# A state-space layer and a feed-forward layer on one core: the weight splits of all eight W_out blocks by ScalarE copies and adding transfers, and a new order from entry 201 on

## The chip, the core and the metric

The kernel runs on one core of one Trainium2 chip. A core has a matrix engine (TensorE; the profile shows its matmuls as PE and its weight loads as PEld), three engines for elementwise work (VectorE or DVE, ScalarE or ACT, GpSimd or POOL) and a synchronising engine (SyncE or SP) that issues most of the transfers. All of them work side by side, each through its own queue in order, and wait for one another by semaphores. The metric is the device time of one execution in microseconds. The kernel before took 329.49 us (median of 3 runs, 328.6 to 329.88).

## What is computed

The reference chains two layers. The first is a state-space scan over 4 batches, 8 heads and 768 positions in float32 (head width 32, state width 16). It works in chunks; within a chunk

```python
M = CB * L                       # L = exp(cum[i] - cum[j]), causal
y_intra = np.einsum('bhij,bhjd->bhid', M, xc)
y_inter = np.einsum('bhin,bhnd->bhid', Cc, state) * decay_to_i[:, :, :, None]
y[:, :, sl] = y_intra + y_inter
state = decay_full[:, :, None, None] * state + np.sum(Bx, axis=2)
```

The result, 3072 tokens of 256 numbers, goes through the second layer, with W_in of 256 x 2048 and W_out of 2048 x 256:

```python
h = x @ w_in
g = h * (1.0 / (1.0 + np.exp(-h)))
return (g @ w_out).astype(np.float32)
```

## The kernel before

**Units and groups.** The scan is cut into twelve units of 256 tokens (u = 0 to 11, three in each batch), and the feed-forward layer into six groups of two units (G or P = 0 to 5). Each weight matrix is cut into eight blocks of 128 x 2 x 256 numbers: blocks 0 to 7 are W_in, blocks 8 to 15 are W_out.

**Split weights.** From group 1 on the feed-forward matmuls run on numbers of a narrower float type, fp32r, and to keep float32 accuracy each weight block and each activation is split into three parts: a high part (`h`), a low part (`l`) and a third part (`d`). For a block n, `lw` loads it, `u` and `v` (ScalarE) and `w` (VectorE, three steps, `w,n,0` to `w,n,2`) and `W` (GpSimd adds, line 318) make the rounded word, `H` (ScalarE, line 322) the high part. The low and third parts can be made in two ways. Either VectorE does both: `lD` (line 326) adds high part and word, `dD` (line 330) makes the third part of high and low part. Or ScalarE and the transfers do: `Wl` and `Wd` (line 335) are ScalarE copies of the high part, plain and scaled, into the places of the low and the third part; `Wm` (line 339) is a transfer, issued from GpSimd's queue, that adds the word onto the low part, and `We` one that adds the low part onto the third. `We` of a block therefore waits until the `Wm` of that block has landed, and GpSimd stands still meanwhile. Before the change blocks 12 to 15 have both parts made by copies and transfers, blocks 10 and 11 the low part only, and blocks 8 and 9 neither: ten transfers.

**The order.** Nothing is scheduled when the kernel is built: a string, `SCHEDULE` (lines 18 to 100), lists 1309 entries such as `q,1,0,1,0`, and a loop at the end of the kernel calls the function of each entry with its numbers. An engine's queue is the entries of that engine in the order of the string. A second table, `SLOTS` (lines 102 to 116), says which place in a pool of equal buffers the next tile of that pool takes (49 places `s2k` of 2 KB a partition, 12 `r4k` of 4 KB, 7 `raw`, 3 PSUM banks `hp`). A tile that takes a place waits until the last user of that place has finished.

**Entries that the text speaks of.** Of the scan: `La`, `Lp`, `Ln`, `Lt`, `Lx` load a unit's inputs (SP); `E` (VectorE scan, line 512), `T` (VectorE transposition of loaded B or C, line 525), `B` and `C` (GpSimd, lines 520 and 551), `ce` (ScalarE, line 546) prepare the operands of `g0` (PE, line 585) and `gd` (PE, line 571); `M` (VectorE, line 600) uses what `g0` made; `b` (ScalarE, line 594) copies what `gd` made, and the four `S` (VectorE, line 615) carry the state over it, `SM` (ScalarE, line 623, twice a unit) masks the states, and `Y` (PE, lines 635 and 644) needs `SM`, `M` and `C`. `y`, `xh` (ScalarE, lines 672 and 679) and `x` (VectorE) then split the result for the feed-forward layer. `AA`, `AP`, `AD` make the decay tables that `La` and `Lp` read; they are on GpSimd except `AP` (VectorE, line 486).

Of the feed-forward layer: group 0 uses plain float32 matmuls for part of its work, `s` (line 697) with `si` (ScalarE, line 703) for W_in and `n1` (line 761) for W_out; an `n1` needs the finished word of its W_out block, an `s` that of its W_in block. With split weights, `a,G,i` (PE, line 800) multiplies by high and low part of block i, `ax` (ScalarE, line 811) rescales the sum in PSUM, `d` (PE, line 800) adds the third part, `dg` (ScalarE, line 821) applies the activation; `h` (ScalarE, line 827), `l` and `e` (VectorE, lines 651 and 837) split the activation, and `q,P,i,k,m` (PE, line 782) is three matmuls by the high, low and third part of W_out block 8 + i, in this order. Scan and feed-forward share two PSUM tiles, `ga` and `gb`. Results are turned by `o` (VectorE, line 715) and stored by `O` (SP).

Of the kernel before, what the change touches and what calls it, by code (L numbers as in the profile page):

```python
# [888 lines left out]
```

## Time and profile before

| what | time |
|---|---|
| median of the three runs | 329.49 us |
| the runs | 328.6, 329.49, 329.88 us |
| the profiled execution | 329.1 us |
| its span, first to last instruction | 327.4 us |
| time around the span (difference) | 1.7 us |
| granted TensorE clock over the span | 0.999 |

The span is the time in which the profile shows instructions. A busy share is the time in which an engine has at least one instruction in work; a PE that is busy all the time has another matmul started before the last has left it. Rows of grouped instructions give the source line, the engine, the operation, what it writes and reads, how often it occurs, its busy time in us and the mean of one in ns. Rows of the stretches give, for a stretch of time, the us in which PE, PEld, DVE, ACT and POOL were busy, with the count of instructions, the granted clock, the share of the 16 DMA engines and GB/s. Rows of the chain of waits and of the timeline begin with the start in us and the duration in us, and end with a count.

### The profile page before, as it was taken

To read this page: it belongs to the slowest core of one execution; us is meant where nothing else is said; L and a number is where in the kernel's file an instruction comes from. 1 tells how busy PE (TensorE), PEld (TensorE's weight loads), DVE (VectorE), ACT (ScalarE), POOL (GpSimd) and SP (SyncE) were. 2 spreads that over 40 slices of the span, in tenths; PEclk is the share of its full clock that TensorE was granted. 3 is DMA by queue.
4 is the path that set the end of the run, shared out by engine and by line. 5 is a ranking of instruction groups with operands and counts; after the bars stand their busy time and mean duration, and the time that the engine had idled before them with its cause. 6 is when DMAs were issued, how large, how long until landed. Compare 5 with 4: busy or idle time off the path is not lost.

```text
span 327.4 us, 7519 instructions
## 1 busy us (share of the span) xinstructions
PE 320.3 (98%) x3064; PEld 243.4 (74%) x3067; DVE 240.4 (73%) x331; ACT 209.5 (64%) x319; POOL 56.0 (17%) x74
## 2 busy tenths in 40 slices
...
GB/s 162 206 200 272 296 175 192 51 148 135 148 127 46 105 115 53 86 36 64 147 74 70 44 1 117 104 26 96 3 74 37 7 2 2 0 88 0 2 1 64
DMA packets 94962, 29.27 MB, mean 89 GB/s; under 512 B 80000, under 2 KB 86912, under 8 KB 94928
## 3 DMA queue, kind: packets, MB, share of 16 engines
...
## 4 chain that ended last, share of the span: by engine, by line
PE 94%; SPq 2%; DMA 1%; DVE 1%; issue 1%; DVEq 0%
PE hp L782 29%; PE ga L800 18%; PE gb L800 18%; PE hp L761 9%; PE hp L697 6%; PE o_ps L782 6%; PE ga L635 2%; PE ga L585 2%; PE ga L644 2%; DMA s2k<-in_C_dram 1%; PE gb L644 1%; PE ga L571 1%; SPq L262 0%; SPq L375 0%; PE o_ps L531 0%
## 5 line engine op out<-in xcount | busy, mean ns | idle before, releaser
L782 PE MATMUL hp<-r4k,s2k 128*128 128x512 f32 x400 | 110.0, 394 | 0.0
L651 DVE SCALAR_TENSOR_TENSOR r4k<-r4k,r4k 128x1024 fp32r<-128x1024 f32 (+1 forms) x42 | 50.5, 1202 | 51.3 <-ACT r4k L827 48.2
L782 PEld LDWEIGHTS hp<-r4k,s2k 128*128 128x128 f32 x400 | 74.0, 188 | 16.4 <-issue 0.3
L800 PE MATMUL ga<-raw,s2k 128*128 128x512 f32 x240 | 62.3, 395 | 0.0
L800 PE MATMUL gb<-raw,s2k 128*128 128x512 f32 x240 | 61.1, 390 | 0.0
L800 PEld LDWEIGHTS ga<-raw,s2k 128*128 128x128 f32 x240 | 44.7, 188 | 11.4 <-ACT ga L811 0.9
L800 PEld LDWEIGHTS gb<-raw,s2k 128*128 128x128 f32 x240 | 44.8, 188 | 9.9 <-ACT gb L811 0.5
L837 DVE SCALAR_TENSOR_TENSOR r4k<-r4k,r4k 128x1024 fp32r<-128x1024 f32 x40 | 49.2, 1231 | 3.4 <-DVE r4k L651 0.9
L827 ACT ACTIVATE r4k<-r4k 128x1024 fp32r<-128x1024 f32 x40 | 42.2, 1058 | 3.2 <-issue 1.3
L811 ACT ACTIVATE ga<-ga 128x1024 f32<-128x1024 f32 x21 | 21.1, 1007 | 24.6 <-PE ga L800 23.8
L811 ACT ACTIVATE gb<-gb 128x1024 f32<-128x1024 f32 x21 | 21.2, 1009 | 17.6 <-PE gb L800 13.3
L782 PE MATMUL o_ps<-r4k,s2k 128*128 128x512 f32 x80 | 30.7, 390 | 0.0
L761 PE MATMUL hp<-r4k,s2k 128*128 128x512 f32 x64 | 30.0, 602 | 0.0
L821 ACT ACTIVATE r4k<-gb 128x1024 f32<-128x1024 f32 x21 | 21.4, 1021 | 12.4 <-PE gb L800 9.9
L520 POOL TENSOR_TENSOR BT<-bn,ab 128x256 f32<-128x256 f32 x10 | 6.7, 672 | 129.5 <-DVE ab L512 123.3
L318 POOL TENSOR_TENSOR s2k<-s2k,s2k 128x512 uint32<-128x512 uint32 (+1 forms) x19 | 23.6, 1250 | 26.4 <-DVE s2k L307 13.7
L821 ACT ACTIVATE r4k<-ga 128x1024 f32<-128x1024 f32 x21 | 21.5, 1023 | 8.4 <-PE ga L800 8.2
L512 DVE TENSOR_TENSOR_SCAN ab<-ab,diag 128x512 f32<-128x512 f32 x20 | 24.8, 1265 | 0.0
L697 PE MATMUL hp<-r4k,s2k 128*128 128x256 f32 x96 | 22.3, 382 | 0.2 <-issue 0.2
L697 PEld LDWEIGHTS hp<-r4k,s2k 128*128 128x128 f32 x96 | 18.0, 190 | 4.0 <-issue 1.4
L761 PEld LDWEIGHTS hp<-r4k,s2k 128*128 128x128 f32 x64 | 11.6, 189 | 10.5 <-issue 9.6
L782 PEld LDWEIGHTS o_ps<-r4k,s2k 128*128 128x128 f32 x80 | 15.0, 188 | 3.2
...
## 6 DMA issues: line engine op xcount, KB each, us to landing
ab<-az SPq DMA_DIRECT2D x20, 256.0 KB, 4.2
...
s2k<-s2k POOLq DMA_DIRECT2D x10, 256.0 KB, 3.8
...
```

The source lines that it names most:

```text
L318: nc.gpsimd.tensor_tensor(out=u[:, :, fs], in0=u[:, :, fs], in1=v[:, :, fs], op=ALU.add)
L512: nc.vector.tensor_tensor_scan(out=o, data0=src, data1=diag.rearrange("p h t -> p (h t)"), initial=0.0, op0=ALU.mult, op1=ALU.add)
L644: nc.tensor.matmul(out=y[w][32 * q:32 * q + 32, c, 64 * k:64 * k + 64], lhsT=xc[64 * c:64 * c + 64, k, h], rhs=m[64 * c:64 * c + 64, k, h] ...
L651: nc.vector.scalar_tensor_tensor(out=l, in0=f32(h), scalar=BACK, in1=y, op0=ALU.mult, op1=ALU.add)
L697: nc.tensor.matmul(out=hp[:, i], lhsT=WT[j][:, kc, 128 * i:128 * i + 128], rhs=XM()[:, 2 * kc:2 * kc + 2, u], start=(kc == 0), stop=(kc == ...
L761: nc.tensor.matmul(out=NP[m], lhsT=WT[8 + f // 2][:, f % 2, 128 * m:128 * m + 128], rhs=GT[0, f // 2][:, f % 2], start=(n == 1), stop=(n = ...
L782: nc.tensor.matmul(out=ACC[P, c], lhsT=WK[8 + i, p][:, k, 128 * m:128 * m + 128], rhs={"h": HT, "l": LT, "d": DT}[p][P, i][:, k], start=(n ...
L800: nc.tensor.matmul(out=o, lhsT=WK[j, q][:, kc, 128 * i:128 * i + 128], rhs=xs[:, 2 * kc:2 * kc + 2], start=(start and q == "h" and kc == 0 ...
L811: nc.scalar.activation(t, t, AF.Copy, scale=1.0 + Z)
L821: nc.scalar.activation(g, t, AF.Silu, scale=BACK)
L827: nc.scalar.activation(t, GT[G, i], AF.Copy, scale=-LESS * Z)
L837: nc.vector.scalar_tensor_tensor(out=DT[G, i], in0=f32(HT[G, i]), scalar=-1.0, in1=f32(LT[G, i]), op0=ALU.mult, op1=ALU.subtract)
```

## The change

Entries 1 to 200 of the order stay. From there on the order is a new one until some 180 us into the execution; the last 323 entries are again those of before. What is done differently in it: the VectorE steps `lD,8`, `lD,9`, `dD,8`, `dD,9`, `dD,10` and `dD,11` are gone, and `Wl,8`, `Wd,8`, `Wl,9`, `Wd,9`, `Wd,10` and `Wd,11` (ScalarE copies) and `Wm,8`, `We,8`, `Wm,9`, `We,9`, `We,10` and `We,11` (adding transfers) take their place. All eight W_out blocks now get low and third part by copies and transfers: sixteen transfers instead of ten. No other work is added or removed; loads, matmuls and stores are the same ones, in another order on every queue. `SLOTS` is changed from the 80th place of `s2k`, the 15th of `r4k`, the 17th of `raw` and the 16th of `hp` on, so that the new order finds free places. No function is changed.

The diff of the order up to the last adding transfer, and of one table of places:

```diff
--- before.py
+++ after.py
@@ -25,94 +25,94 @@
 ce,1,0 g0,1 Lx,1,1,0 Lx,1,0,0 W,4 xh,0 w,5,1 si,0,0 B,1,0 P01,1,1 D,1 s,0,4 M,1,1 lw,1 u,1 lw,12 S,1,0 W,5 v,1 ca S,1,1
 S,1,2 SM,1,0 SM,1,1 lw,13 s,0,5 si,0,5 v,12 C,1 M,1,0 Y,1 w,1,0 w,1,1 W,7 si,0,4 lw,8 w,1,2 W,1,0 z,1 w,12,2 X0,1,0 H,7
 S,1,3 X0,1,1 x,0,0 lD,7 u,12 w,12,0 w,12,1 u,13 w,13,0 w,13,1 W,1,1 s,0,1 u,8 v,8 s,1,5 ir,3 w,8,0 si,0,1 s,1,0 co
-Ln,2,0,1,0 xh,1 W,12 x,1,0 w,8,1 v,13 w,13,2 W,13 lw,15 u,15 w,8,2 Ln,2,1,1,0 si,1,5 s,1,4 a,0,7 si,1,4 n1,9,0 H,12
-Wd,12 x,0,1 lw,14 u,14 n1,11,0 n1,9,1 x,1,1 W,8 Ln,2,1,0,0 v,14 w,14,2 ir,0 si,1,0 n1,1,0 n1,1,1 H,0 n1,0,1 H,1 lw,6 v,6
-w,6,2 n1,11,1 n1,10,1 ir,2 ir,1 u,6 lw,10 Wl,12 AA,0 AA,1 AD,4 w,6,0 AP w,6,1 AD,0 lw,2 Ln,2,0,0,0 ax,0,7 w,15,0 u,10
-u,2 W,6 n1,8,0 AD,1 v,2 H,6 v,10 w,2,0 s,1,1 si,1,1 lw,3 tp,2 dD,7 v,3 v,15 u,3 w,2,1 w,2,2 W,2,0 Lt,3,1,3,0 lD,6 dD,6
-w,14,0 n1,8,1 w,3,2 a,0,6 ax,0,6 w,15,2 W,2,1 s,1,2 si,1,2 H,2 d,0,7 w,14,1 dg,0,7 AD,2 w,3,0 w,15,1 d,0,6 dg,0,6 W,14
-Lt,3,1,0,0 w,10,2 s,0,2 lw,9 u,9 v,9 Lt,3,1,2,0 Lt,3,1,1,0 T,3,1 H,4 si,0,2 n1,10,0 Lx,2,0,0 n1,12,1 La,2,0,0 w,3,1 tq,2
-La,2,1,0 E,2,1 E,2,0 lD,4 w,9,0 W,15 n1,15,1 Lt,3,0,0,0 n1,12,0 B,2 ce,2,0 ce,2,1 Lt,3,0,3,0 g0,2 lw,11 u,11 Lp,2,0 C,2
-M,2,1 Lx,2,1,0 gd,2 b,2,0 b,2,1 S,2,0 S,2,1 H,15 S,2,2 W,3 Lp,3,0 Lt,4,1,1,0 H,13 La,3,1,0 w,10,0 v,11 Lt,4,1,0,0
-n1,15,0 SM,2,0 Wl,15 SM,2,1 w,10,1 W,10 ce,3,1 Lt,4,1,3,0 M,2,0 La,3,0,0 E,3,1 E,3,0 s,0,3 si,0,3 Lt,3,0,2,0 ce,3,0
-n1,13,0 Lt,3,0,1,0 T,3,0 Y,2 Lx,3,1,0 Ln,3,0,0,0 y,2,0 y,2,1 xh,2 x,2,0 n1,5,0 x,2,1 Ln,3,0,1,0 s,1,3 w,9,1 g0,3 C,3 B,3
-M,3,1 Lx,3,0,0 gd,3 b,3,0 b,3,1 S,3,0 S,3,1 Lt,4,0,1,0 w,9,2 n1,0,0 n1,14,1 Lx,4,0,0 Lt,4,0,0,0 La,4,0,0 S,3,2 W,9
-n1,13,1 SM,3,0 M,3,0 SM,3,1 lD,0 Y,3 n1,2,1 n1,3,0 Lt,4,0,3,0 dD,0 La,4,1,0 w,11,0 w,11,1 y,3,0 y,3,1 xh,3 x,3,0 w,11,2
-n1,2,0 W,11 H,10 a,1,0 Wl,10 Wm,10 n1,3,1 n1,4,0 Lt,4,1,2,0 T,4,1 x,3,1 si,1,3 S,3,3 Lp,4,0 C,4 ce,4,1 E,4,0 H,11 ax,1,0
-d,1,0 E,4,1 ce,4,0 Lt,4,0,2,0 n1,5,1 Wl,11 Lx,5,1,0 Wl,13 dg,1,0 n1,4,1 T,4,0 H,8 lD,1 Ln,4,0,0,0 g0,4 lD,2 Ln,4,0,1,0
-B,4 H,9 M,4,1 La,5,1,0 Wm,11 Lx,4,1,0 Wm,12 gd,4 b,4,0 lD,8 b,4,1 dD,1 n1,6,1 h,1,0 S,4,0 S,4,1 Lx,5,0,0 H,3 S,4,2
-SM,4,1 n1,14,0 n1,6,0 SM,4,0 Lt,5,1,3,0 M,4,0 n1,7,0 Vn,0 Y,4 y,4,1 y,4,0 xh,4 l,1,0 n1,7,1 S,4,3 a,1,2 Vn,1 lD,9 dD,8
-dD,2 H,5 a,1,1 ax,1,2 e,1,0 q,1,0,1,0 d,1,2 dD,9 q,1,0,0,1 Ln,5,0,0,0 ax,1,1 d,1,1 Wd,13 Lt,5,1,1,0 q,1,0,0,0 q,1,0,1,1
-AD,3 Lt,5,1,0,0 dD,4 dg,1,2 Lt,5,0,3,0 h,1,2 a,1,4 dg,1,1 h,1,1 Lt,5,1,2,0 T,5,1 ce,5,0 Lt,5,0,2,0 ce,5,1 Lt,5,0,0,0
-lD,3 a,1,3 Lp,6,0 dD,10 o,0,1,2 We,12 dD,3 x,4,1 x,4,0 l,1,2 e,1,2 ax,1,4 d,1,4 H,14 q,1,2,0,1 Ln,5,0,1,0 ax,1,3 d,1,3
-l,1,1 La,5,0,0 E,5,0 dg,1,4 e,1,1 q,1,1,1,1 dg,1,3 Lt,5,0,1,0 h,1,3 q,1,1,0,1 E,5,1 T,5,0 g0,5 B,5 M,5,1 Lp,5,0 C,5 gd,5
-b,5,1 lD,5 Lt,6,1,0,0 b,5,0 S,5,0 Lt,6,1,3,0 S,5,1 Wm,13 We,13 dD,5 q,1,2,1,1 La,6,0,0 q,1,2,0,0 a,1,5 Lx,6,1,0 Wl,14
-ax,1,5 M,5,0 q,1,1,1,0 l,1,3 S,5,2 q,1,1,0,0 SM,5,1 dD,11 La,6,1,0 e,1,3 SM,5,0 d,1,5 h,1,4 dg,1,5 h,1,5 o,0,0,2
-Lt,6,1,2,0 Lt,6,1,1,0 T,6,1 q,1,2,1,0 l,1,4 e,1,4 q,1,3,0,0 l,1,5 e,1,5 q,1,3,1,0 Wd,15 Y,5 E,6,1 Lt,6,0,1,0 y,5,0 y,5,1
-xh,5 q,1,3,1,1 q,1,3,0,1 ce,6,0 Lt,6,0,0,0 a,1,7 ce,6,1 q,1,4,0,0 q,1,5,1,0 Lt,6,0,3,0 ax,1,7 q,1,4,1,0 Lt,7,1,1,0 Wm,15
-We,15 d,1,7 q,1,4,1,1 dg,1,7 Lt,6,0,2,0 Wd,14 q,1,5,1,1 E,6,0 q,1,5,0,1 T,6,0 h,1,7 g0,6 Ln,6,0,1,0 x,5,0 Lx,6,0,0
-Ln,6,0,0,0 B,6 La,7,1,0 M,6,1 gd,6 b,6,1 Lt,7,1,0,0 x,5,1 Wm,14 M,6,0 q,1,4,0,1 a,2,1 b,6,0 ax,2,1 a,1,6 ax,1,6 S,6,0
-S,6,1 Lt,7,0,0,0 C,6 S,6,2 l,1,7 e,1,7 SM,6,1 S,6,3 d,2,1 dg,2,1 SM,6,0 q,1,7,1,0 We,14 d,1,6 dg,1,6 h,1,6 q,1,5,0,0
...
+Ln,2,0,1,0 xh,1 W,12 x,1,0 w,8,1 v,13 w,13,2 W,13 lw,15 u,15 H,0 s,1,4 si,1,4 si,1,5 w,8,2 Ln,2,0,0,0 W,8 lw,2 a,0,7
+n1,9,1 ax,0,7 v,2 si,1,0 u,2 n1,9,0 dD,7 ir,0 x,1,1 H,1 n1,10,0 ir,2 ir,1 AA,0 H,12 Wl,12 n1,1,1 n1,0,1 lw,6 v,6 u,6
+n1,1,0 w,2,0 n1,10,1 w,15,0 w,15,1 w,2,2 AD,4 Lt,3,1,2,0 x,0,1 w,6,0 w,6,1 v,15 n1,8,0 w,15,2 AA,1 AP AD,0 H,5 w,6,2
+n1,8,1 W,6 d,0,7 w,2,1 W,2,1 lw,3 u,3 v,3 w,3,2 w,3,0 s,1,1 Ln,2,1,1,0 Wd,12 lD,0 lw,14 u,14 si,1,1 H,6 H,13 lD,6 v,14
+dg,0,7 n1,11,0 Ln,2,1,0,0 W,2,0 Lt,3,1,1,0 w,14,0 lw,10 tp,2 n1,11,1 Lx,2,0,0 u,10 s,1,2 v,10 si,1,2 w,3,1 W,15 ce,2,1
+H,15 n1,15,0 dD,6 tq,2 La,2,0,0 a,0,6 AD,1 n1,0,0 ce,2,0 ax,0,6 n1,14,0 Wl,13 w,10,0 d,0,6 dg,0,6 H,8 W,3 w,14,1 s,0,2
+w,10,1 si,0,2 La,2,1,0 E,2,1 E,2,0 w,14,2 B,2 Lx,2,1,0 lw,9 u,9 g0,2 Lt,3,1,3,0 v,9 Lt,3,1,0,0 T,3,1 gd,2 b,2,0 b,2,1
+Lp,2,0 C,2 s,0,3 w,10,2 W,14 M,2,1 M,2,0 S,2,0 S,2,1 W,10 w,9,0 La,3,0,0 La,3,1,0 n1,15,1 n1,12,1 ce,3,0 Wd,8 H,10 S,2,2
+SM,2,0 SM,2,1 ce,3,1 n1,5,0 w,9,2 si,0,3 H,4 Ln,3,0,0,0 Wl,8 E,3,0 lw,11 Lt,3,0,1,0 u,11 n1,4,0 w,9,1 W,9 H,3 Y,2 y,2,0
+E,3,1 Lt,4,1,0,0 Lt,3,0,3,0 Lt,3,0,2,0 y,2,1 Ln,3,0,1,0 xh,2 Lt,3,0,0,0 T,3,0 B,3 Lx,3,0,0 s,1,3 si,1,3 Wd,13 x,2,0 g0,3
+M,3,1 Lx,3,1,0 gd,3 b,3,0 Lp,3,0 H,2 b,3,1 S,3,0 La,4,0,0 n1,12,0 w,11,0 n1,3,0 Lt,4,1,3,0 S,3,1 S,3,2 SM,3,0 SM,3,1 C,3
+n1,2,0 M,3,0 Y,3 n1,14,1 x,2,1 w,11,1 v,11 w,11,2 W,11 Wl,15 Wm,15 n1,13,0 y,3,1 y,3,0 n1,7,1 Wd,15 xh,3 Ln,4,0,1,0
+Lt,4,1,2,0 Lt,4,1,1,0 lD,4 T,4,1 x,3,0 a,1,0 lD,5 Lx,4,0,0 H,9 n1,7,0 n1,2,1 Lt,4,0,3,0 Wd,9 H,11 x,3,1 dD,0 ce,4,1
+ax,1,0 d,1,0 ce,4,0 La,4,1,0 E,4,0 S,3,3 E,4,1 Lp,4,0 C,4 AD,2 dg,1,0 n1,4,1 H,14 Wd,14 Wl,9 n1,6,0 La,5,1,0 Ln,4,0,0,0
+B,4 Lt,5,1,0,0 Lt,4,0,1,0 Lt,4,0,0,0 Lt,4,0,2,0 T,4,0 g0,4 M,4,1 Lx,4,1,0 gd,4 b,4,0 n1,3,1 S,4,0 lD,2 La,5,0,0 b,4,1
+S,4,1 Wm,8 Wl,10 Wm,12 S,4,2 SM,4,0 SM,4,1 n1,6,1 Wl,11 Ln,5,0,1,0 n1,5,1 M,4,0 Y,4 y,4,0 y,4,1 xh,4 E,5,0 n1,13,1 h,1,0
+Lp,5,0 lD,1 a,1,1 ax,1,1 Vn,1 a,1,2 ax,1,2 dD,1 E,5,1 d,1,1 dg,1,1 La,6,0,0 Lt,5,1,2,0 h,1,1 l,1,0 e,1,0 We,8 Lt,5,0,2,0
+q,1,0,0,0 Wm,9 We,9 dD,2 d,1,2 x,4,1 dg,1,2 lD,3 dD,3 q,1,0,1,0 a,1,3 Wd,10 Vn,0 Lt,5,0,0,0 ax,1,3 x,4,0 Lx,5,0,0 Wm,10
+a,1,4 l,1,1 Lt,5,1,1,0 h,1,2 AD,3 d,1,3 q,1,0,0,1 ax,1,4 Lt,5,1,3,0 T,5,1 dD,4 e,1,1 dg,1,3 Ln,5,0,0,0 d,1,4 S,4,3
+q,1,1,1,0 Wd,11 ce,5,1 ce,5,0 Wm,11 l,1,2 e,1,2 q,1,1,1,1 Lt,5,0,3,0 q,1,1,0,1 B,5 q,1,1,0,0 Lt,6,1,0,0 dg,1,4 h,1,4
+Lt,5,0,1,0 T,5,0 q,1,0,1,1 l,1,4 g0,5 Lx,5,1,0 M,5,1 gd,5 b,5,1 b,5,0 We,10 q,1,2,1,1 q,1,2,0,0 h,1,3 q,1,2,0,1
+Lt,6,1,2,0 a,1,5 Lt,6,0,1,0 We,12 e,1,4 q,1,4,1,0 La,6,1,0 l,1,3 q,1,4,1,1 Lt,6,0,3,0 We,11 Lt,6,1,3,0 dD,5 Lt,6,1,1,0
+ax,1,5 d,1,5 e,1,3 Lp,6,0 dg,1,5 q,1,3,0,1 S,5,0 S,5,1 S,5,2 SM,5,0 q,1,4,0,1 q,1,4,0,0 Lt,6,0,0,0 SM,5,1 Wm,13 h,1,5
+M,5,0 E,6,0 C,5 Y,5 y,5,1 We,13 Lt,6,0,2,0 T,6,1 Lx,6,0,0 ce,6,0 C,6 y,5,0 xh,5 q,1,3,1,0 a,1,7 Wl,14 Wm,14 l,1,5 e,1,5
+q,1,5,1,1 q,1,5,0,0 x,5,0 Lx,6,1,0 Ln,6,0,1,0 ax,1,7 ce,6,1 E,6,1 d,1,7 dg,1,7 q,1,3,1,1 q,1,3,0,0 Ln,6,0,0,0 B,6 gd,6
+T,6,0 g0,6 M,6,1 Lx,7,1,0 We,14 b,6,1 q,1,5,1,0 b,6,0 S,6,0 M,6,0 S,6,1 q,1,2,1,0 S,6,2 La,7,0,0 a,2,1 x,5,1 a,1,6 h,1,7
+q,1,5,0,1 l,1,7 e,1,7 La,7,1,0 E,7,0 E,7,1 ax,2,1 d,2,1 Lt,7,0,3,0 SM,6,1 ax,1,6 SM,6,0 d,1,6 We,15 Lt,7,1,0,0 q,1,7,0,1
...
 SLOTS = {
     "s2k": """
 0 1 2 3 4 6 7 5 8 9 10 11 12 13 14 15 16 17 18 19 20 21 22 23 24 25 26 27 28 29 30 31 32 33 34 35 36 37 38 39 40 41
-42 43 44 45 46 47 48 4 1 9 3 6 11 12 14 8 0 15 19 10 20 26 18 16 22 5 7 24 27 21 2 28 23 30 31 39 37 38 1 47 48 6 44
-17 0 8 12 18 13 27 9 29 3 34 36 5 26 15 25 35 40 43 45""",
+42 43 44 45 46 47 48 4 1 9 3 6 11 12 14 8 0 15 19 10 20 26 18 16 22 5 7 24 27 21 2 28 23 30 31 39 37 46 38 4 13 1 42
+9 11 10 26 24 37 40 17 25 43 36 34 29 7 6 20 23 35 8 41""",
...
```

96 lines of the change are left out of this document (48 added, 48 removed), and 6 rows, old and new, of the table SLOTS.

## The prediction

> **What bounds the kernel now.** I read the page's busy times and the shares of the chain of waits first, then the stretches of time, then the groups of the steps that change.
>
> ```profile
> span 327.4 us, 7519 instructions
> PE 320.3 (98%) x3064; PEld 243.4 (74%) x3067; DVE 240.4 (73%) x331; ACT 209.5 (64%) x319; POOL 56.0 (17%) x74
> PE 94%; SPq 2%; DMA 1%; DVE 1%; issue 1%; DVEq 0%
> ```
>
> ```profile
> 20.00:30.00 10.00, 9.72 (x193) 8.15 (x193) 8.76 (x20) 7.54 (x16) 5.49 (x9) 1.00 0.97 289
> 30.00:175.00 145.00, 145.00 (x1492) 106.18 (x1491) 123.28 (x165) 102.22 (x167) 40.00 (x43) 1.00 0.58 116
> 70.00:80.00 10.00, 10.00 (x108) 5.70 (x89) 9.62 (x13) 8.59 (x15) 4.30 (x6) 1.00 0.94 145
> 80.00:90.00 10.00, 10.00 (x170) 6.27 (x155) 9.85 (x18) 6.50 (x14) 2.49 (x4) 1.00 0.86 147
> 90.00:100.00 10.00, 10.00 (x46) 8.28 (x45) 8.68 (x11) 9.33 (x12) 0.00 (x0) 1.00 0.65 104
> 100.00:110.00 10.00, 10.00 (x96) 7.79 (x95) 8.93 (x15) 6.71 (x11) 3.81 (x5) 1.00 0.35 63
> ```
>
> The matrix engine is 94% of the chain. From 30 to 175 us, which is the stretch that the new order covers, it is busy for 145.00 of 145.00 us at the full granted clock (1.00); the only idle time near it is 10.00 - 9.72 = 0.28 us between 20 and 30 us. VectorE is nearly as full from 70 to 90 us (9.62 and 9.85 of 10), and so are the transfers (0.94 and 0.86), but PE waits for neither. The change leaves PE's work as it is. So what it can gain is at most that 0.28 us, and each us by which some operand comes late after it is lost, because no idle time of PE follows that could take it up.
>
> **The change part by part.** The removed and the added steps, by groups:
>
> ```profile
> L326 DVE TENSOR_TENSOR s2k<-s2k,s2k 128x512 fp32r<-128x512 f32 x10 | 7.5, 756 | 0.0
> L330 DVE SCALAR_TENSOR_TENSOR s2k<-s2k,s2k 128x512 fp32r<-128x512 f32 x12 | 8.4, 715 | 0.1
> L335 ACT ACTIVATE s2k<-s2k 128x512 fp32r<-128x512 f32 x10 | 6.2, 625 | 0.1
> L339 POOL DMA_DIRECT2D s2k<-s2k x10 | 8.8, 935 | 12.9 <-DMA s2k<-s2k 5.8 <-ACT s2k L335 3.7 <-issue 3.4
> ```
>
> *VectorE* loses two low parts and four third parts, 2 x 0.756 + 4 x 0.715 = 4.4 us, all between 81 and 108 us in the old order. Worth 0: PE was not waiting. The range's end on this side is the 0.28 us above.
>
> *ScalarE* gains six copies, 6 x 0.625 = 3.8 us. From 70 to 110 us it is busy for 8.59 + 6.50 + 9.33 + 6.71 = 31.1 of 40 us; with the copies it would be 34.9, so I cost them at 0. The cover is thin between 90 and 100 us (9.33): there a copy ahead of an `ax` or `dg` would cost PE up to its own 0.63 us.
>
> *GpSimd* gains six issues, 6 x 0.935 = 5.6 us, beside 10.6 us of work in those 40 us. The issues are no load, but each `We` makes the queue wait until its `Wm` has landed.
>
> *The transfers* gain six of 256 KB:
>
> ```profile
> q0 software_dynamic: 608, 1.07, 21.6%
> s2k<-s2k POOLq DMA_DIRECT2D x4, 256.0 KB, 4.9
> DMA to landing us min/median/max: 3.3/3.8/5.9
> 78.62 0.64 POOL L520 TENSOR_TENSOR BT<-bn,ab 128x256 f32<-128x256 f32 x1 [2.48 <-DVE ab L512]
> 79.20 1.78 POOL L339 DMA_DIRECT2D s2k<-s2k  x2
> 80.34 1.27 POOL L470 DMA_DIRECT2D ac<-r4k  x1
> 85.01 0.88 POOL L339 DMA_DIRECT2D s2k<-s2k  x1 [3.40 <-DMA s2k<-s2k]
> ```
>
> The first two rows are of the stretch from 70 to 100 us: the software queue took 21.6% of 30 us = 6.5 us of all 16 engines, nearly all for four adding transfers, 1.6 us each, and they landed 4.9 us after their issue (median); over the whole run it is 3.3 to 5.9, median 3.8. Six more are 6 x 1.6 = 9.7 us. From 80 to 110 us the engines were busy for 8.6 + 6.5 + 3.5 = 18.6 us; the new order makes this 28 of 30. I therefore count with 4.9 us, the value of the crowded stretch.
>
> Now the chain that the change makes. In the new order GpSimd's queue behind `B,4` is `Wm,8 Wm,12 We,8 Wm,9 We,9 Wm,10 AD,3 Wm,11 B,5 We,10`. `B,4` waits for VectorE's `E,4`, as the first row of the timeline shows, and ends at 79.3, so `Wm,8` leaves at 79.2 and lands at 84.1. `We,8` follows about 0.5 us later at 84.6 (the old `We,12` left at 85.0 after the same kind of wait) and lands at 89.5; `Wm,9` leaves behind it at 85.5, lands at 90.4; `We,9` leaves at 90.9, `Wm,10` at 91.8 and lands at 96.7; `We,10` leaves at 97.2 and lands at 102.1. Who needs them: `q,1,0,0,0` for its third matmul, `Wd,11` (it takes the place that `Wm,10` reads from, and stands on ScalarE ahead of `ce,5` and `dg,1,4`, for which `g0,5` waits), and `q,1,2,1,1`. For PE's dates:
>
> ```profile
> 66.46 2.77 PE hp L761 x6
> 80.57 3.63 PE hp L761 x8
> 90.17 0.84 PE L782 MATMUL hp<-r4k,s2k 128*128 128x512 f32 x3
> 102.35 0.30 PE ga L585 x2
> L546 ACT ACTIVATE ce<-ct,par 128x256 f32<-128x256 f32 x20 | 9.5, 500 | 0.3 <-DVE ct L525 0.3
> L821 ACT ACTIVATE r4k<-ga 128x1024 f32<-128x1024 f32 x21 | 21.5, 1023 | 8.4 <-PE ga L800 8.2
> ```
>
> In the old order the first `q` begins at 90.17. In the new one a `d` (four matmuls, about 0.9 us) stands ahead of it and one `n1` less (0.9) ahead of `Y,4`, so it is due at about 90.2 to 90.6 and its third matmul 0.4 later, at 90.8: 1.3 us after 89.5. `g0,5` is at 102.35 in the old order and within 0.5 us of it in the new; the first `q,1,2` follows one us later, its third matmul at 103.8, 1.7 us after 102.1. `Wd,11` must begin by 102.35 - 1.02 - 2 x 0.50 - 0.63 = 99.7, 3.0 after 96.7. At 4.9 us a landing the chain costs 0; at 3.3 it has 5 us in hand; at 5.9 each of the four landings in a row is 1.0 later, 4.0 in all, and `q,1,2,1,1` is late by 4.0 - 1.7 = 2.3 us. I take 0.1, being nearest to the row of the crowded stretch, and keep 0 and 2.3 for the range.
>
> The Trainium skill prices such a transfer in its page "DMA: Bandwidth & Descriptors", section "Anatomy of one DMA — SWDGE (gpsimd) path": about 2.0 us fixed and the bytes by 436 GB/s, an estimate of 2.6 us for 256 KB. The trace's smallest is 3.3 and its median 3.8, so the measurement decides; by the page the chain would end 9 us earlier and this term would be 0 instead of 0.1.
>
> The rest is order. Two places of it are packed closer than before. First `Y,4`:
>
> ```profile
> 80.36 0.69 DVE L600 TENSOR_TENSOR ab<-gb,ab 128x512 f32<-128x512 f32 x1
> 82.17 1.00 DVE L615 SCALAR_TENSOR_TENSOR st<-st,pfx,bxs 128x64 f32<-128x64 f32 x3
> 83.20 0.69 ACT L623 ACTIVATE sm<-st,par 128x128 f32<-128x128 f32 x2 [0.60 <-DVE st L615]
> 84.20 0.20 PE ga L635 x2
> ```
>
> Between `gd,4` and `Y,4` PE had four `n1` (3.63 us from 80.57), then `Y,4` at 84.20, 0.3 after the `SM` pair ended at 83.89. The new order leaves it three `n1`: by the row of three, 2.77 us, PE is free at 83.34. VectorE then goes `M,4,1` (to 81.05), three `S` (1.00) with `lD,2` (0.76) between them, to 82.8; the `SM` pair 0.69 and a hand-over make 83.6. PE waits 0.3 us. Bounds: 0 if VectorE starts earlier, 0.6 with `Wl,10` in the way on ScalarE.
>
> Second `s,1,2`, which needs both halves of `W,2`:
>
> ```profile
> 39.51 1.23 DVE L486 TENSOR_TENSOR_SCAN r4k<-r4k,r4k 48x520 f32<-48x520 f32 x1
> 41.05 0.63 POOL L470 DMA_DIRECT2D ac<-r4k  x1 [1.68 <-DVE s2k L307]
> 41.70 1.28 POOL L318 TENSOR_TENSOR s2k<-s2k,s2k 128x512 uint32<-128x512 uint32 x1
> 44.89 2.27 POOL L318 TENSOR_TENSOR s2k<-s2k,s2k 128x256 uint32<-128x256 uint32 x2 [1.38 <-DVE s2k L310]
> 47.91 1.73 PE hp L697 x8
> L307 DVE TENSOR_SCALAR s2k<-s2k 128x512 uint32<-128x512 uint32 x16 | 9.4, 585 | 0.2
> L303 DVE TENSOR_SCALAR s2k<-s2k 128x512 f32<-128x512 f32 x16 | 8.9, 559 | 0.5 <-ACT s2k L294 0.5
> ```
>
> GpSimd now does `AD,0`, `W,6` and the halves directly behind `AP`: 0.63 + 1.28 + 2.27 = 4.2 us. `AP` ended at 40.7; ahead of it VectorE now has five short steps more (net): `dD,7`, two first and two second `w` steps, 0.715 + 2 x 0.559 + 2 x 0.585 = 3.0 us. So it ends at about 43.7 and the halves at 47.9, where `s,1,2` is due. I take 0.1, between 0 and 0.5.
>
> Elsewhere I found the operands ahead of PE by 0.1 us and more; for such joints that turn out short I add 0.3 (0 to 1.0, each at most a few tenths like the two above). Sum: 0 + 0 + 0.1 + 0.3 + 0.1 + 0.3 = +0.8 us. Against the profiled execution's 329.1 us (span 327.4 and 1.7 around it) that is 329.9; the median of the runs is 0.4 higher, 329.5, so I predict 330.3 us, within the 0.5% (1.65 us) that I take as the least change that a measurement of this kernel tells from none.
>
> **The rivals.** *The chain of landings becomes the path* (slower). `Wm,8`, `Wm,9`, `Wm,10`, `We,10` in a row on GpSimd, in a stretch whose transfers go from 18.6 to 28 of 30 us. It decides from a landing time of 4.9 + 1.7/4 = 5.3 us on; at 5.9 the price is 2.3 us and the time 330.3 + 2.3 = 332.6. For it: one landing of 5.9 us lies in the run already, with fewer transfers in flight, and the chain starts where the transfers are busy for 0.86 of the time. Against it: the median over the run is 3.8, and up to 5.3 the queue's reserve takes it up.
>
> *The loads of unit 5 come late* (slower). `La,6,0` now stands in SP's queue ahead of most of unit 5's `Lt`, and it must wait until `Y,4` has freed its buffer, at 85.6, when the next matmuls begin. Six `Lt` follow one by one, the last at about 89.
>
> ```profile
> 85.61 1.06 PE hp L761 x2
> 89.16 0.66 DVE L525 STREAM_TRANSPOSE ct<-tbc 128x256 f32<-128x256 f32 x1
> DMA to landing us min/median/max: 3.0/3.0/4.3
> ```
>
> They landed in 3.0 to 4.3 us between 60 and 112, so by 93.3 now. The old `T,5,1` ran at 89.16; the new one stands behind `l,1,1`, `x,4,0` and `dD,3`, which by the matmuls that these wait for I estimate at 94, and nothing that PE needs soon is queued behind it for some 2.5 us. So a landing later than about 96.5, 7.5 us after the issue, reaches PE, one us for one; at twice the 4.3, with 0.5 us more for the issue, it costs 1.6 and the time is 331.9.
>
> *VectorE's relief reaches PE* (less time): 4.4 us freed where VectorE is 96 to 98% busy. Nothing in the rows of the stretches has PE waiting there, so its price is the 0.28 us and a few joints of 0.1: 329.0.
>
> **How the numbers follow.** The forecast 0.60; the chain of landings 0.23; the loads 0.10; the relief 0.07, of which 0.03 would be more than 0.5%, for a cause that the rows hide. Same: 0.60 + 0.04 = 0.64; slower 0.33; faster 0.03. The low end, 328.8, is the relief with a good median; the high end, 333.0, is the chain at 5.9 us a landing with 0.4 more in the joints.
>
> **What would show it.** Right: PE busy for all but about 0.8 us between 30 and 175 us, VectorE's busy time down by some 4 us and ScalarE's up by 3.8, L339 sixteen times, `g0,5` within a us of 102.35, and everything behind 180 us shifted by one constant. Wrong: a wait of PE's weight loads on L339's landings or on ScalarE around `q,1,0`, `g0,5` or `q,1,2` (first rival); VectorE waiting on tbc near 94 us (second); PE's start of `q,1,0` earlier than 90 us (third). A longer landing, over 5.3 us in the median of 80 to 100 us, is what would make the prediction wrong.

## The result, and the profile after

The changed kernel took 331.6 us (median of 6 runs, 330.4 to 332.31), the kernel before beside it 329.36 us (6 runs, 328.6 to 329.88): a ratio of 1.0066, 95% interval 1.0041 to 1.0091. It is slower, by 0.66%. A later comparison with more runs (the first experiment below) gave 331.28 us over 12 runs against 329.89 over 35, ratio 1.0034, interval 1.0014 to 1.0055. The medians differ by 2.24 and by 1.39 us. The prediction was 330.3 us with a range of 328.8 to 333.0, and "within 0.5%" as the likeliest case.

The profiled execution after is the longest of its six runs: 332.31 us, span 330.6. The head of its page, the software queue, the shares of its chain of waits, and the row of the adding transfers:

```profile
span 330.6 us, 7544 instructions
...
PE 320.4 (97%) x3067; PEld 243.1 (74%) x3067; DVE 233.3 (71%) x325; ACT 212.2 (64%) x325; POOL 64.5 (20%) x80
...
q0 software_dynamic: 2480, 4.39, 7.8%
...
PE 82%; DMA 7%; SPq 4%; POOL 3%; ACT 2%; issue 1%; DVE 0%; DVEq 0%; POOLq 0%
...
s2k<-s2k POOLq DMA_DIRECT2D x16, 256.0 KB, 5.0
```

VectorE lost 7.1 us of busy time (240.4 to 233.3), ScalarE gained 2.7, GpSimd 8.5, and PE's 320.4 us are the 320.3 of before. So the 3.2 us by which the span grew are waits of PE. The rows of the stretches say where. First those of the kernel before, the stretch up to 30 us included, then those of after; the second number is PE's busy time:

```profile
0.00:30.00 30.00, 27.38 (x409) 17.97 (x413) 24.05 (x58) 19.27 (x40) 12.09 (x26) 1.00 0.86 213
```

```profile
0.00:30.00 30.00, 26.30 (x407) 16.99 (x408) 22.73 (x56) 18.64 (x38) 12.13 (x25) 1.00 0.95 227
30.00:175.00 145.00, 142.90 (x1431) 104.44 (x1430) 113.99 (x156) 103.43 (x171) 47.74 (x49) 1.00 0.60 120
175.00:320.00 145.00, 145.00 (x1205) 117.08 (x1204) 92.70 (x108) 88.58 (x115) 4.64 (x7) 1.00 0.24 42
```

PE stood still 1.08 us longer before 30 us (27.38 - 26.30), 2.10 us between 30 and 175 us, and not at all behind it: 3.18 of the 3.2 us. The first 1.08 us lie in the 200 entries that both kernels have in common. Over the twelve profiles of the experiments, all with the same 200 entries, PE's busy time up to 30 us goes from 25.15 to 27.15 us. The start of `s,1,4`, PE's first entry of the new order, scatters less, from 31.52 to 32.75 us, against 31.59 in the profile of before and 32.65 in that of after. So this part goes up and down by 1 to 2 us from one execution to the next, and the one profile of before is at the good end of it. What the change itself does in this execution is in the 2.10 us. PE's waits between 30 and 175 us in the kernel after, and VectorE's between 76 and 86 us (who waited, for whom, us in total, times, longest):

```profile
PE ga L585 <- DVE bh L525: 1.4, 1, 1.4
PE hp L697 <- POOL s2k L318: 0.6, 1, 0.6
```

```profile
DVE bh L525 <- DMA tbc<-in_B_dram: 2.4, 1, 2.4
```

Two joints. The second row is `s,1,2`, which waits for a half of `W,2`. The first is `g0,4`: it waits for `T,4,0`, which itself waits 2.4 us for the B loads of unit 4. SP's queue and GpSimd's show why both are late. SP after (start, length of the issue):

```profile
66.38 0.59 SPq L229 DMA_DIRECT2D ab<-az  x1
...
72.65 0.59 SPq L229 DMA_DIRECT2D ab<-az  x1
73.29 0.61 SPq L237 DMA_DIRECT2D pfx<-ac  x1
74.01 0.59 SPq L229 DMA_DIRECT2D ab<-az  x1
74.64 0.59 SPq L254 DMA_DIRECT2D bn<-in_B_dram  x1
75.33 0.53 SPq L262 DMA_DIRECT2D tbc<-in_C_dram  x1
75.91 2.00 SPq L262 DMA_DIRECT2D tbc<-in_B_dram  x3
```

The three B loads `Lt,4,0` of the last row left at 75.9 to 77.0 us. Before, the first of them left at 64.40. In the new order they stand behind `La,4,0,0` (66.38), which had waited 2.4 us for its place, and behind `La,4,1,0` and `La,5,1,0`. The last of them landed 5.9 us after its issue, and `T,4,0` began at 83.03. GpSimd after and before, in the stretch ahead of `s,1,2`:

```profile
44.86 0.73 POOL L470 DMA_DIRECT2D ac<-r4k  x1 [4.55 <-DMA ab<-az]
45.62 5.58 POOL L318 TENSOR_TENSOR s2k<-s2k,s2k 128x512 uint32<-128x512 uint32 x4
```

GpSimd stands idle for 4.55 us until `AP` is done (this row names a transfer as what ended the wait; the same row of e0_after names line 486 of VectorE, which is `AP`), issues `AD,0`, and then runs four adds without a break: `W,6`, the two halves `W,2,1` and `W,2,0`, `W,15`. The halves end at 49.5 us. PE was ready for `s,1,2` 0.65 us earlier.

### The profile page after: what moved, and what is told of

Read it like the earlier page. It is cut to its first block, busy times and chain, and to the rows that moved or that the text cites. A ratio compares the mean times of both kernels' runs of the same rounds, so it can differ in the third digit from the quotient of the medians.

```text
span 330.6 us, 7544 instructions
## 1 busy us (share of the span) xinstructions
PE 320.4 (97%) x3067; PEld 243.1 (74%) x3067; DVE 233.3 (71%) x325; ACT 212.2 (64%) x325; POOL 64.5 (20%) x80
## 4 chain that ended last, share of the span: by engine, by line
PE 82%; DMA 7%; SPq 4%; POOL 3%; ACT 2%; issue 1%; DVE 0%; DVEq 0%; POOLq 0%
PE hp L782 28%; PE ga L800 17%; PE gb L800 17%; PE o_ps L782 6%; PE hp L761 4%; PE hp L697 3%; DMA s2k<-in_B_dram 2%; POOL s2k L318 2%; DMA tbc<-in_B_dram 2%; PE ga L585 2%; PE ga L635 1%; PE ga L644 1%; DMA tbc<-in_C_dram 1%; PE ga L571 1%; SPq L262 1%; DMA ab<-az 1%
## 5 line engine op out<-in xcount | busy, mean ns | idle before, releaser
L318 POOL TENSOR_TENSOR s2k<-s2k,s2k 128x512 uint32<-128x512 uint32 (+1 forms) x19 | 26.3, 1397 | 22.4 <-DVE s2k L310 9.8
L339 POOL DMA_DIRECT2D s2k<-s2k x16 | 14.7, 1031 | 20.9 <-DMA s2k<-s2k 16.3
```

What stands on the lines that cost most here:

```text
L318: nc.gpsimd.tensor_tensor(out=u[:, :, fs], in0=u[:, :, fs], in1=v[:, :, fs], op=ALU.add)
L339: nc.gpsimd.dma_start(out=f32(WK[n, p]).rearrange("p k f -> p (k f)"), in_=other.rearrange("p k f -> p (k f)"), accum_op=ALU.add)
```

## The experiments

The twelve kernels were run in three groups, each group beside the kernel before on one chip. In the table, "idle" is 145.00 minus PE's busy time from 30 to 175 us in the profile of that run.

| run | median us | beside it, before | ratio (95%) | idle |
|---|---|---|---|---|
| e0_after | 331.28 | 329.89 | 1.0034 (1.0014 to 1.0055) | 0.66 |
| e1_loads | 330.88 | 329.89 | 1.0026 (1.0005 to 1.0047) | 0.66 |
| e2_w2 | 331.76 | 329.89 | 1.0067 (1.0044 to 1.0091) | 1.66 |
| e3_both | 331.48 | 329.89 | 1.0053 (1.0033 to 1.0072) | 1.66 |
| e4_w2early | 331.19 | 329.41 | 1.0045 (1.0019 to 1.0071) | 1.18 |
| e5_w2early_loads | 331.1 | 329.41 | 1.0054 (1.0030 to 1.0077) | 1.33 |
| e6_order | 334.33 | 329.41 | 1.0138 (1.0113 to 1.0163) | 3.43 |
| e7_transfers | 330.28 | 329.41 | 1.0023 (1.0002 to 1.0044) | 0.00 |
| e8_all | 330.07 | 329.46 | 1.0010 (0.9992 to 1.0029) | 0.00 |
| e9_dg | 330.96 | 329.46 | 1.0042 (1.0027 to 1.0057) | 1.21 |
| e10_w2dg | 329.88 | 329.46 | 1.0022 (1.0006 to 1.0038) | 0.00 |
| e11_twice | 331.06 | 329.46 | 1.0051 (1.0036 to 1.0065) | 0.75 |

### The two joints, one by one

The changed kernel once more, unchanged, as the base.

> The changed kernel once more, beside the kernel before, as the base of the other three. Its measured ratio was 1.0066 (331.6 against 329.36 us); expected again 331.3 to 332.0 us. In the profile at hand the matmuls of entry s,1,4, which stands in both kernels behind the same 200 entries, begin 1.06 us later than before. If that is the jitter of one execution (a load of 64 KB that landed late at 17 us), this execution shows another number there, between -0.5 and +1.0. What the order itself makes should come again: s,1,2 about 0.7 us later than s,1,4 is, and g0,4 about 1.6 us later than Y,3 is, each against the profile of before; together 2.3 us, which is about the 2.24 us between the medians.

One edit of SP's queue:

```diff
-... La,4,0,0 ... La,5,1,0 ... Lt,4,0,1,0 Lt,4,0,0,0 Lt,4,0,2,0 T,4,0 g0,4
+... Lt,4,0,1,0 Lt,4,0,0,0 Lt,4,0,2,0 La,4,0,0 ... La,5,1,0 ... T,4,0 g0,4
```

> The loads Lt,4,0,1, Lt,4,0,0 and Lt,4,0,2 are put ahead of La,4,0,0 in the queue of SP; nothing else is moved. Theory Q (queue order): g0,4 came 1.6 us late because these loads stood behind La,4,0,0, which waits for its place until Y,2 has ended, and behind La,5,1,0; so they left at 75.9 to 77.9 us instead of 64 to 70. Put ahead, they land before 75 us, T,4,0 waits for VectorE alone, and the kernel gains 1.6 us: 330.0 us, ratio to the kernel before 1.002. Theory L (the landings): the six more transfers and the crowd on the DMA engines between 75 and 84 us make whatever lands there late; then moving the loads only lets other operands of g0,4 come late (La,4, E,4), and the gain is at most 0.3 us: 331.3 us. Theory D: nothing of the change is on the path but the scatter of the first 200 entries: no change, 331.6 us.

One edit of GpSimd's queue:

```diff
-... W,6 d,0,7 w,2,1 W,2,1 lw,3 ... Ln,2,1,0,0 W,2,0 ...
+... d,0,7 w,2,1 W,2,1 W,2,0 W,6 lw,3 ... Ln,2,1,0,0 ...
```

> In the queue of GpSimd the two halves W,2,1 and W,2,0 are put ahead of W,6; nothing else is moved. Theory Q: s,1,2 waits for the halves, which stand behind AP (on VectorE), AD,0 and W,6; W,6 took 2.5 us beside VectorE's steps. With W,6 behind them, s,1,2 begins some 0.7 us earlier, and W,6 and H,6 are early enough (block 6 is first used by a,0,6): 330.9 us, ratio 1.0045. Theories L and D: 331.6 us. Against Q: if the halves wait for VectorE's w,2,1 or for AD,0, not for W,6, the gain is 0.1 us or none.

And both edits.

> Both moves together. Theory Q: the two stalls lie one behind the other on PE, so their prices add: 331.6 - 2.3 = 329.3 us, ratio 1.000, the time of the kernel before. Theory L: 331.0 to 331.6 us. If the gain of each alone is there but their sum is not, the time that they free ends in a next wait, and the profile of this run names it.

*The base.* This time the profile has one wait of PE between 30 and 175 us, and no other. The rows are from e0_after, the stretch and then PE's waits in it:

```profile
30.00:175.00 145.00, 144.34 (x1482) 105.30 (x1484) 116.53 (x157) 104.40 (x172) 48.69 (x49) 1.00 0.60 123
```

```profile
PE hp L697 <- POOL s2k L318: 0.7, 1, 0.7
```

So `s,1,2` is late in every execution of this order that was profiled (0.6 or 0.7 us in after, e0, e1, e6, e9 and e11). `g0,4` is not: here the `Lt,4,0` left 1.1 us earlier (74.81), the last landed 4.6 us after its issue instead of 5.9, and `T,4,0` waited 0.2 us instead of 2.4, which PE did not see. The expectation that g0,4 comes 1.6 us late again was wrong. The loads are at the edge: of the eight profiles that have them where the change puts them, the one of after loses 1.4 us of PE there and the other seven nothing, though `T,4,0` waits for them up to 0.7 us.

*The loads early.* In e1_loads `T,4,0` has no wait, and the stall at `s,1,2` stays (0.7). The median fell by 0.4 us, not by 1.6; the interval of its ratio lies almost wholly over that of the base, so the gain is not shown. Theory Q had the mechanism and took a stall of some executions for one of all.

*W,2 ahead of W,6.* Here theory Q failed. The wait at `s,1,2` is gone as it foretold, but the time did not fall, and PE's idle time rose to 1.66 us. PE's and ScalarE's waits of e2_w2 between 42 and 56 us:

```profile
PE hp L761 <- ACT r4k L821: 1.7, 1, 1.7
```

```profile
ACT s2k L322 <- POOL s2k L318: 2.1, 1, 2.1
```

The next entry, `n1,15,0`, now waits for `dg,0,7` on ScalarE (line 821). `dg,0,7` was not late by itself: in ScalarE's queue it stands behind `H,6` (line 322), and `H,6` waits 2.1 us for `W,6`, which the edit had made later. In the unchanged order this second wait lies hidden behind the first: there ScalarE's idle time ahead of `H,6` is 0.79 us.

*Both.* e3_both has the same single wait of PE as e2_w2 (1.7 us at `n1,15,0`) and 331.48 us. Theory Q expected 329.3 us; it did not come, and the profile names the next wait.

### W,2 in GpSimd's idle time, and which of order and technique costs

```diff
-... w,2,0 n1,10,1 ... AA,1 AP AD,0 H,5 w,6,2 n1,8,1 W,6 d,0,7 w,2,1 W,2,1 ... W,2,0 ...
+... w,2,0 w,2,1 n1,10,1 ... AA,1 W,2,1 W,2,0 AP AD,0 H,5 w,6,2 n1,8,1 W,6 d,0,7 ...
```

> Base: the changed kernel at 331.3 us beside 329.9 for the kernel before, where s,1,2 alone cost 0.8 us in the profile and W,15 came next on GpSimd. Here w,2,1 is put behind w,2,0 on VectorE and the halves W,2,1 and W,2,0 ahead of AD,0 on GpSimd, so that they fill the 4.5 us that GpSimd stood idle for AP, and neither AD,0, W,6 nor W,15 comes later by more than 0.5 us. Theory Q (GpSimd's queue at 44 to 50 us is what the new order costs): s,1,2 and n1,15,0 both go without a wait, the gain is 0.8 us, 330.5 us, ratio 1.0015. Theory T (the transfers cost what is left): 331.3 us, as the stall only moves on. Theory S (AP and with it AD,0 are delayed by the halves and the loss shows at g0,2 or later): 331.3 to 332 us.

> The same, and Lt,4,0,1, Lt,4,0,0 and Lt,4,0,2 ahead of La,4,0,0 in SP's queue. With the loads alone the median fell from 331.28 to 330.88 us and the scatter from 2.4 to 1.5 us, and T,4,0 had no wait, so the late loads cost 1.6 us in some executions and nothing in others. Theory Q: 330.1 us, ratio 1.0000 to 1.0010, with the smaller scatter. Theory T: 330.9 us.

The new order with the technique of before (the six VectorE steps are put where the transfers stood, the six copies are gone):

```diff
-... Wd,8 ... Wl,8 ... Wd,9 ... Wl,9 ... Wm,8 ... We,8 ... Wm,9 We,9 ... Wd,10 ... Wd,11 ... We,10 ... We,11
+... lD,8 ... dD,8 ... lD,9 dD,9 ... dD,10 ... dD,11
```

> The new order with the technique of before: lD,8 and lD,9 on VectorE in the places of Wm,8 and Wm,9, dD,8 to dD,11 in the places of We,8 to We,11; the six copies Wl,8, Wd,8, Wl,9, Wd,9, Wd,10 and Wd,11 and the six transfers are gone. Theory Q: the time is the changed kernel's, 331.3 us (331.0 to 331.6), as nothing on the path is made by the six transfers. Theory T: it falls to 329.9 to 330.3 us.

And the order of before with the technique of after. The cut shows the steps of blocks 8 to 11; `H,11`, `Wl,11`, `Wm,11`, `Wl,13`, `Wd,13`, `We,12`, `AD,3`, `H,14` and `Wl,14` are moved besides, so the queues of ScalarE and GpSimd are not those of before. In this run and in e6_order the table of the places `s2k` is changed to fit.

```diff
-... H,8 lD,1 ... b,4,0 lD,8 b,4,1 ... lD,9 dD,8 ... dD,9 ... dD,10 ... dD,11
+... H,8 ax,1,0 ... Wl,8 Wd,8 ... Wm,8 B,4 ... SM,4,0 We,8 Wl,9 Wm,9 Wd,10 We,12 We,10 ... Wd,9 We,9 ... Wd,11 ... We,11
```

> The order of before with the technique of after: lD,8, lD,9 and dD,8 to dD,11 are taken out, and Wl, Wd, Wm and We of blocks 8 to 11 put in on ScalarE and GpSimd, early enough by the profile of before; H,8 is put ahead of H,11 for it, Wl,11, Wl,13, Wd,13, H,14 and Wl,14 some us later, into gaps of ScalarE. PE, VectorE and SP keep their order. Theory Q: within 0.3 us of the kernel before, 329.9 us. Theory T: 331 us or more. The landing of We,8 (some 87 us by 5 us a transfer) against the first third matmul of block 8 at 90.8 us is the closest joint; if it is late, PE stands still there and the profile shows that wait at the weight loads of q,1,0,1,0.

*W,2 early.* In e4_w2early the halves now run from 41.2 to 43.2 us in GpSimd's gap, and `s,1,2` has no wait. But the loss moves on again. PE's and ScalarE's waits of e5_w2early_loads between 42 and 56 us, and ScalarE's timeline there:

```profile
PE hp L761 <- ACT r4k L821: 1.3, 1, 1.3
```

```profile
ACT s2k L322 <- POOL s2k L318: 1.8, 1, 1.8
```

```profile
45.66 0.60 ACT L703 ACTIVATE r4k<-hp 128x512 f32<-128x512 f32 x1 [1.58 <-PE hp L697]
48.07 1.15 ACT L322 ACTIVATE s2k<-s2k 128x512 fp32r<-128x512 f32 x2 [1.81 <-POOL s2k L318]
49.13 0.66 ACT L297 ACTIVATE s2k<-raw 128x512 f32<-128x512 uint32 x1
49.69 1.01 ACT L821 ACTIVATE r4k<-gb 128x1024 f32<-128x1024 f32 x1
```

ScalarE stands idle for 1.81 us ahead of `H,6` and `H,13` (48.07), and `dg,0,7` (49.69) is the fourth behind that idle time. What `dg,0,7` reads was there before 45 us. The medians (331.19 and 331.1 us) are the changed kernel's: theory Q's gain of 0.8 us did not come, theory T's time did, but not for T's reason, as the next two runs show.

*Order or technique.* With the technique of before the new order is slower still, 334.33 us, 4.9 us above the kernel before. PE's waits of e6_order between 30 and 175 us:

```profile
PE o_ps L782 <- DVE s2k L330: 1.3, 1, 1.3
PE ga L800 <- DVE s2k L330: 1.1, 1, 1.1
PE hp L697 <- POOL s2k L318: 0.7, 1, 0.7
PE ga L635 <- ACT sm L623: 0.3, 1, 0.3
```

Both theories had expected less. The stall at `s,1,2` is there as before, and VectorE's third parts (line 330) now come too late for a `q` and a `d`. The six steps were put where the transfers had stood, so this does not say that no better place exists for them; it says that this order has no room on VectorE at these places, and that the transfers are what makes it run.

The other way round, in e7_transfers, the profile has no wait of PE from 30 to 175 us (145.00 of 145.00), and the time is 330.28 us, ratio 1.0023 with the interval from 1.0002 to 1.0044. Theory T (331 us or more) falls; theory Q's "within 0.3 us" lies inside the interval, but the median is 0.9 us above the kernel before. Some of the 0.9 us may be the technique's: the profile shows only joints of 0.1 to 0.25 us at other places, no wait of a weight load on a landing. The medians alone do not part order from technique, since this interval overlaps that of the base (1.0014 to 1.0055); that the order makes the waits is read from the profiles.

### The head of ScalarE's queue

```diff
-... s,1,1 ... si,1,1 H,6 H,13 lD,6 v,14 dg,0,7 n1,11,0 ...
+... s,1,1 ... si,1,1 dg,0,7 H,6 H,13 lD,6 v,14 n1,11,0 ...
```

Three kernels have this edit: with W,2 early and the loads early (e8), alone (e9), and with W,2 early (e10).

> In both kernels with the halves W,2 early, s,1,2 had no wait any more, but n1,15,0 began 1.3 to 1.5 us late behind it. The profile names dg,0,7 on ScalarE, which ended at 50.7 to 51.1 us; it stands behind H,6, and H,6 waited 1.7 to 1.8 us for W,6 on GpSimd, although what dg,0,7 reads was ready at 44.5 us. Here, beside W,2 early and the loads Lt,4,0 early, dg,0,7 is put right behind si,1,1, ahead of H,6. Theory Q2 (the new order costs its time in the queues of GpSimd and ScalarE at 44 to 51 us, one head of line behind the other, and in SP's queue at 76 us): all of it goes; 331.1 - 1.5 = 329.6 us, ratio 1.000 to 1.001, the time of the kernel before, and the matmul entries from g0,6 on lie within 0.3 us of the kernel before, counted from s,1,4. Theory M (a further operand is late behind it, as twice already): 330.5 to 331.1 us.

> The changed kernel with dg,0,7 alone put behind si,1,1. Theory Q2: s,1,2 still waits for the halves of W,2, so the 0.8 us stay: 331.3 us, and n1,15,0 follows s,1,2 without a wait. If ScalarE alone were the cause, the time falls by 0.8 us to 330.5.

> W,2 early and dg,0,7 behind si,1,1, with the loads where the changed kernel has them. Theory Q2: 329.7 to 330.1 us, and single executions up to 1.6 us longer where T,4,0 waits for its loads; the difference to the run with the loads moved is what the loads cost on average, 0.1 to 0.4 us. Theory M: 331 us.

PE's stretch in e8_all:

```profile
30.00:175.00 145.00, 145.00 (x1492) 105.86 (x1490) 116.80 (x158) 104.97 (x173) 48.59 (x49) 1.00 0.60 121
```

No wait is left, as in the kernel before. e8_all takes 330.07 us, ratio 1.0010 with an interval that holds 1, e10_w2dg 329.88 us. They were expected at 329.6 and 329.7 to 330.1. Counted from `s,1,4`, the last entry's start differs from that of before by +0.15 us in e8 and -0.05 us in e10. Theory M falls. That the waits are gone is shown by the profiles; the gain in time is less sure, because the intervals of both runs overlap that of the base. Alone the edit does nothing that can be measured (e9_dg: 330.96 us, 331.3 expected), as theory Q2 said, since `s,1,2` still waits 0.7 us; this execution also lost 0.5 us at `a,1,0`, which waited for the split of unit 3's result (line 651), a wait that no other profile has and whose cause stays open.

The loads moved or not made no difference that the medians show (330.07 with, 329.88 without); seven of eight profiles had lost nothing there. Neither kernel beats the kernel before.

### How much cover the chain of landings has

```diff
-... e,1,0 We,8 Lt,5,0,2,0 ...
+... e,1,0 We,8 We,8 Lt,5,0,2,0 ...
```

> The changed kernel with We,8 issued twice, one behind the other, so that the low part of block 8 is added onto its third part a second time (the third part of that block, and only that, is therefore another number). The second must wait for the landing of the first, so all later transfers of the chain come some 5 us later. In the profile of the changed kernel We,8 landed at 90.3 us and the third matmul of q,1,0,0,0 begins at 93.2, so 2.9 us of cover. Theory C (the chain of landings has a cover of some 3 us, and costs nothing as it is): PE waits 2.0 to 2.5 us at the third matmul of q,1,0,0,0 and no more later; 333.5 us. Theory L (the landings are on the path already): 336 us. Theory H (whatever the transfers do is hidden by other work): 331.3 us.

GpSimd's timeline in e11_twice:

```profile
81.10 1.79 POOL L339 DMA_DIRECT2D s2k<-s2k  x2
85.22 0.84 POOL L339 DMA_DIRECT2D s2k<-s2k  x1 [2.32 <-DMA s2k<-s2k]
89.45 1.72 POOL L339 DMA_DIRECT2D s2k<-s2k  x2 [3.40 <-DMA s2k<-s2k]
96.08 1.73 POOL L339 DMA_DIRECT2D s2k<-s2k  x2 [4.91 <-DMA s2k<-s2k]
```

The second `We,8` left at 89.45 and landed at 93.25 us, 3.8 us later; the base had its only one landed at 90.33. So the delay was 2.9 us, not 5. PE's rows of `q,1,0,0,0` and of the `d` behind it, in the base and then in e11_twice:

```profile
92.52 0.84 PE L782 MATMUL hp<-r4k,s2k 128*128 128x512 f32 x3
93.20 1.07 PE L800 MATMUL ga<-raw,s2k 128*128 128x512 f32 x4
```

```profile
92.67 1.18 PE L782 MATMUL hp<-r4k,s2k 128*128 128x512 f32 x3
93.69 1.09 PE L800 MATMUL ga<-raw,s2k 128*128 128x512 f32 x4
```

In the base the third of the three matmuls begins at 92.97 us, 2.6 us behind the landing. In e11_twice the `q` begins 0.15 us later than in the base and the `d` 0.49 us later: the weight load of the third matmul began at 93.35, just behind the landing, the matmul at 93.38, and 0.34 us were lost. PE's idle time shows only 0.09 of it (0.75 against 0.66), because the second matmul was still in work. So the cover is about 2.6 us, near the 2.9 that theory C had read, and what goes beyond it is lost on PE. Theory L (336 us) falls. Theory H falls as a mechanism, though its time came (331.06 us): the two landings were short (3.9 and 3.8 us), and 0.3 us is less than the scatter of the medians.

## Why the prediction was right and wrong

**What bounds the kernel: right.** PE is the bound, and each late operand is lost one for one: 3.18 us of idle time against 3.2 us of span in the profile after. VectorE's busy time fell by 7.1 us (5.4 in the base, 4.4 foretold) and no part of it came back as time. The rival that VectorE's relief reaches PE is refuted.

**VectorE, worth 0: right for the old order, and too narrow for the new.** Taking the six steps off VectorE in the old order (e7) gains nothing. Putting them back in the new one (e6) costs some 3 us more than the changed kernel has (1.0138 against 1.0034 and 1.0066). The relief is used up by the order. The prediction priced the steps against the old order alone.

**ScalarE, GpSimd and the transfers, worth 0 by themselves: right.** The six transfers took 7.8% of 330.6 us less 5.1% of 327.4 us, 9.1 us of all 16 engines, against 9.7 worked out. ScalarE's busy time rose by 2.7 us, less than the 3.8 of the six copies. No wait of PE in the base or after goes back to a copy or to an issue.

**The chain of landings, 0.1: right.** Landings in the base had a median of 5.1 us from 80 to 110 us (3.4 to 6.9), against the 4.9 counted. `We,8` landed at 90.3 (89.5 foretold) and `We,10` at 102.8 (102.1). No wait of PE goes back to a landing in the base or in after, and e11 shows why: the base has 2.6 us of cover at `q,1,0,0,0`. The prediction had counted 1.3, with the third matmul at 90.8; it began at 92.97 in the base, and `g0,5` at 104.40 instead of near 102.35, because the new order puts more of PE's work ahead of them. So the cost was right and PE's dates were about 2 us early. From 80 to 110 us the median landing in the profile after was 5.4 us, above the 5.3 from which the rival was to decide, and PE did not wait; from 80 to 100 us, the stretch that the prediction named, it was 4.8 (5.1 in the base). The rival did not happen; its point of decision was set too low, as PE's dates were.

**`Y,4`, 0.3: wrong.** No wait of PE stands there in the base or in the profile after. The term was 0.

**`s,1,2`, 0.1 between 0 and 0.5: right place, too small.** It measured 0.65 us. `AP` ended at 44.05 in the base (43.7 foretold) and the halves at 49.00 (47.9 foretold). The step that failed is the sum 0.63 + 1.28 + 2.27 = 4.2 us of GpSimd's work behind `AP`: it was 0.73 + 2.52 + 0.73 + 0.72 = 4.7, because `W,6` took 2.52 us instead of 1.28, of which the shorter halves (1.45 instead of 2.27) gave 0.8 back. The rest of the 1.1 us is `AP`'s 0.35 and the 0.3 us from `AP`'s end to the issue of `AD,0`, which the sum did not have. And the step saw one waiter only. `dg,0,7` behind `H,6` on ScalarE, 0.5 to 1.0 us worse once `s,1,2` is mended, was not in it. The text priced ScalarE's queue by its share of busy time, not by what stands behind a step that waits for GpSimd.

**Other joints, 0.3 (0 to 1.0): wrong in one place.** The second rival, that loads come late because an `La` that waits for its place stands ahead of `Lt` in SP's queue, was the right mechanism at the wrong unit. It was worked out for unit 5, where no wait was seen. It struck unit 4, 1.4 us of PE in one profile of the unchanged new order and nothing in the other. The row that would have shown it was the list of SP's issues from 64 us on, which the prediction did not walk through for unit 4.

**The sum.** +0.8 us was foretold. The base has 0.66 us of PE's idle time, all at `s,1,2`, where 0.1 was foretold; 0.7 of the 0.8 us were put where nothing was lost. That the total of the idle time fits is luck. The medians are 1.39 and 2.24 us above the kernel before. The profile after, of the longest of its executions, has 1.4 us more at the loads of unit 4; how much of that is in the median of its six is not shown. The profile of the base is of an execution of 330.3 us, 1.0 below its median, so what the median has beyond the 0.66 us cannot be read from it. The kernels with no wait at all (e8, e10, e7) still lie 0.4 to 0.9 us above the kernel before. Behind `s,1,4` the profiles of e8 and e10 show at most 0.15 us of it, so in these executions the rest lies ahead of the first entry that was moved; only one profile of before was kept, and what makes the rest stays open. "Within 0.5%" was the likeliest by 0.64 to 0.33, and the first measurement, 0.66%, came out on the other side; the second, 0.34%, did not.

**What would show it.** Everything behind 180 us was shifted by one constant, as foretold (1.2 to 1.4 us in the base). PE's idle time of some 0.8 us was 0.66 in the base and 2.10 in the profile after. `g0,5` was to lie within a us of 102.35 and came at 104.40.
